# Five full-array pairs, joint normalization of two heads, bf16 beta1, alpha2 folded into the first weights, and a new order table, in a block-sparse attention and MLP kernel

## The chip, the cores and the metric

The kernel runs on one core of a Trainium2 chip. The metric is the device time of one execution in microseconds (us). The engines are TensorE (PE; PEld is its weight load), VectorE (DVE), ScalarE (ACT), GpSimd (POOL) and SyncE (SP). Before the change three runs gave 309.32, 309.18 and 308.26 us.

## What is computed

Block-sparse attention (4 batches, 8 heads, 768 tokens, head size 64, blocks of 32 tokens) is followed by a residual MLP that mixes first tokens and then channels:

```python
scores = scale * np.matmul(q, k.transpose(0, 1, 3, 2))
mask = np.abs(blk_i - blk_j) <= window      # window = 1
mask = mask | (blk_i == 0) | (blk_j == 0) | (blk_i == n_blocks - 1) | (blk_j == n_blocks - 1)
# and three sampled key blocks for each query block
scores = np.where(mask, scores, -1000000000.0)
attn = softmax(scores);  x = attn @ v        # x: [4, 768, 512], the heads side by side
a1 = alpha1 * x + beta1
u = x + lam * np.einsum('ts,bsd->btd', w_tok, a1)
a2 = alpha2 * u + beta2
out = u + lam * (np.maximum(a2 @ w_ch1, 0.0) @ w_ch2)   # w_ch1: 512 x 2048, w_ch2: 2048 x 512
```

## The kernel before, in words

**Work units.** The 32 heads form 16 pairs, four to a batch. Scores are computed transposed (keys on the partitions, queries along the free axis), in 9 units for each pair, so there are 144 units. A unit is 1024 columns in two PSUM banks. Unit n belongs to pair n // 9.

**The order table.** The whole program is the string `ORDER`. Each word is one step: letters for the kind, a number for the instance, and after a colon a PSUM bank (for `q`, a pair of banks) or an engine (`a` ScalarE, `d` VectorE). The loop at the end issues the words one after the other, `pin_order` keeps that order on every engine, and `bank_order` adds the waits between engines that reuse of a PSUM bank needs. So an engine never passes a step of its own that still waits. DMA steps stand in the queue of the engine that issues them: loads on POOL, transposes, mask and output on SP.

**Attention words.** `lq lk lv` load q, k, v of a pair with a cast to 16 bits (POOL, L402); six buffers rotate, and loads of pairs from `HELD` on wait for a flag that `F` sets on VectorE (L400). `cq ck cv` cast or regroup them (L517, L532). `q` makes the scores of a unit. For the first `NPE` = 6 pairs ("full array", L585) one head at a time is contracted over 88 rows: 64 of the head and 24 that carry the block mask, so the mask costs nothing later. Those q and k are transposed by TensorE (`H`, L335) and copied out of PSUM (`hq hk`). For the later pairs ("row-tiled", L595) the two heads of the pair run at the same time in the two halves of the array, 64 rows each. There q and k are transposed by DMA on SP's queue (`tq tk`, L554) and the mask is put on after the exp by a minimum with `maskT` on VectorE (`m`, L612). `M N O` make that mask: `N` writes it to DRAM, `O` reads it back, both on SP. `e` is the exp on ScalarE (L605), unit 0 in two halves. `p` and `r` multiply with the values of the first and the second head of the pair (L619); `n` divides by the row sums (a reciprocal, L650, and a multiplication, L653) and writes x into `x_sb`.

**Token mixing.** `lt W w` load and transpose w_tok. `a` and `b` (or by halves `ah`, `bh`) make lam * (alpha1 * x + beta1) (L674, L680). `k` is the matmul (18 of 128x128, L704), `x` adds it to x (L713).

**Channel MLP.** `u` makes alpha2 * u in bf16 (L720). `U` transposes it: by TensorE for batch 0 (L740, with `v` as the copy out of PSUM), by DMA on SP's queue after that (L734). `lw` loads w_ch1 (`w1b`), `lx` and `S` load w_ch2 and scale it by lam. `f` is one block of 128 hidden units for half a batch (four matmuls, L758); f0 to f31 belong to batch 0, whose first 16 carry beta2 along as a further column, copied into `b1t`. `g` is the relu with that bias, on ScalarE (L772) or VectorE (L774). `h` is a quarter of an output block (four matmuls, L792), `o` adds u (L802), `s` stores it (L811).

**Filling.** `z` words are matmuls with zeros into a bank that nobody reads (L298). There are 18 in the table, 7,498 columns in all, all of them ahead of f0. Seven of 512 columns and some small ones stand ahead of the table.

**The start.** Ahead of the table the first pair's q and k are cast, transposed by TensorE into banks 0 and 1, and copied out in halves by VectorE and ScalarE (the last is L359); the mask rows are made beside it.

Of the kernel before, what the change touches and what calls it, by code (L numbers as in the profile page):

```python
# [21 lines left out]
D = 64  # L22
# [3 lines left out]
DM = 512  # L26
# [11 lines left out]
NPE = 6  # L38
# [8 lines left out]
lv0 lq1 lk1 cq0 q0:1 lv1 q1:2 hm0 e0 H1:0 lq2 hq1:d e1 lk2 z512:6 z512:6 q2:1 hk1:d lt0 e2 z512:6  # L47
z512:6 q3:2 cv0 lt1 p0:7 p1 e3 q4:1 lt2 cq1 p2 e4 lv2 z393:6 q5:2 p3 lc0 e5 ck1 z422:6 q6:1 H2:0 lc1
p4 e6 q7:2 hq2:d lc2 n0 e7 z512:6 z498:6 q8:1 lq3 hk2:d r4:7 r5 lv3 e8 r6 cq2 q9:2 cv1 lk3 H3:0 ck2
e9 r7 hq3:d q10:1 lc3 r8 hk3:d e10 lc4 q11:2 n1 H4:0 lq4 W0:1 e11 hq4:d q12:1 lk4 p9:7 hk4:d p10 e12  # L50
q13:2 w0:d H5:0 e13 p11 hq5:d q14:1 p12 hk5:d e14 W1:1 q15:2 w1:d p13 W2:0 e15 n2 q16:1 W3:1 cv2 e16
r13:7 q17:2 w2:d lv4 r14 r15 w3:d e17 W4:0 lw0 L0 q18:1 lw1 r16 w4:a L1 q19:2 lw2 r17 e18 a0 W5:0
lw3 e19 n3 z512:6 z246:6 q20:1 b0 p18:7 e20 z374:6 q21:2 p19 a1 e21 z422:6 q22:1 p20 cq3 e22 z422:6
q23:2 b1 lq5 p21 e23 z422:6 q24:1 ck3 p22 cq4 lk5 H6:1 e24 n4 q25:2 lv5 hq6:d z470:6 r22:7 e25 r23
q26:1 hk6:d r24 w5:a ck4 H7:1 cv3 q27:2 lq6 hq7:d e26 r25 k0:0 lk6 hk7:d e27 cv4 q28:1 L2 lv6 H8:1
x0 e28 q29:2 lx0 hq8:d r26 k1:0 hk8:d e29 lx1 n5 q30:1 q31:2 x1 e30 H9:1 u0 p27:7 p28 hq9:d hk9:a
p29 lx2 q32:1 u1 p30 e31 k2:0 a2 e32 q33:2 M0 x2 U0:1 N0 e33 p31 q34:1 b2 k3:0 v0:a n6 q35:2 e34 x3
r31:7 r32 r33 ah6 O0 k4:0 e35 u2 bh6 q36:1 q37:2 x4 e36 r34 u3 r35 k5:0 e37 n7 q38:1 u4 q39:2 x5 e38
U1:1 ah7 p36:7 p37 v1:a u5 q40:1 p38 bh7 e39 U2:0 cq5 k6:1 v2:d lq7 e40 ck5 k7:0 B0 lk7 x6 cv5 q41:1
u6 lv7 q42:2 e41 x7 H10:1 lx3 p39 cq6 p40 hq10:a u7 z184:6 q43:1 n8 U3:0 hk10:a v3:d z189:6 r40:7  # L60
e42 r41 z384:6 H11:1 ck6 f0:0 cv6 hq11:a hk11:d q44:2 g0:d r42 e43 f1:1 S0 f2:0 e44 g1:d q45:1 g2:a
r43 q46:2 S1 tq6 tk6 r44 e45 f3:0 S2 f4:1 n9 e46 q47:1 g3:d p45:7 g4:a q48:2 a4 p46 e47 f5:0 cq7
f6:1 e48 g5:d q49:1 p47 g6:d e49 q50:2 p48 b4 f7:0 e50 q51:1 ck7 p49 g7:d k8:1 e51 n10 q52:2 tq7 tk7
q53:1 x8 e52 r49:7 r50 cv7 r51 u8 h0:6 e53 S3 q54:0 q55:2 S4 e54 r52 r53 S5 h1 e55 n11 q56:0 q57:1
e56 F24 m54 k9:4 lq8 m55 e57 p54:7 f8:5 x9 p55 m56 q58:0 q59:1 g8:a f9:4 m57 e58 p56 F25 f10:5 u9
lk8 g9:a a5 U4 p57 f11:0 g10:a f12:1 m58 g11:a f13:4 b5 p58 g12:a f14:5 g13:d h2 e59 g14:d k10:4 m59
q60:0 q61:1 cq8 x10 e60 p59 k11:5 ck8 u10 tq8 tk8 e61 f15:4 m60 x11 q62:0 q63:1 g15:a m61 p60 f16:5
e62 F26 u11 lv8 p61 f17:4 g16:a S6 e63 f18:5 g17:d m62 f19:4 g18:a m63 q64:0 q65:1 g19:a p62 S7 U5
f20:5 e64 n12 f21:4 g20:a h3 F27 m64 lq9 g21:a cv8 r54:7 r55 r56 o0 e65 r57 r58 r59 r60 r61 r62
q66:0 q67:2 s0 n13 e66 f22:2 m65 p63:7 p64 e67 f23:3 g22:d p65 h4:6 m66 g23:a m67 q68:0 q69:1 q70:2  # L70
a6 e68 p66 p67 h5 F28 e69 b6 lk9 h6 e70 m68 h7 m69 q71:0 q72:1 q73:2 m70 e71 p68 o1 p69 p70 e72 F29
h8:6 cq9 s1 lv9 m71 e73 k12:0 m72 ck9 p71 k13:1 m73 tq9 tk9 n14 f24:2 x12 r63:7 r64 g24:a r65 r66
x13 r67 r68 r69 r70 r71 ah14 f25:0 n15 h9 g25:a bh14 p72:7 q74:0 q75:1 q76:2 ah15 e74 F30 bh15 p73
lq10 h10 u12 e75 k14:0 m74 e76 u13 k15:1 x14 U6 m75 p74 f26:0 u14 p75 f27:2 g26:a x15 h11 m76 g27:a
u15 q77:0 q78:2 o2 e77 U7 p76 f28:2 F31 cv9 lk10 f29:3 e78 cq10 s2 g28:d f30:0 g29:a m77 f31:1 g30:a
m78 p77 h16:6 g31:a q79:0 q80:1 q81:2 e79 F32 p78 lv10 h17 e80 m79 f32:0 ck10 e81 p79 f33:1 m80 tq10
tk10 f34:2 g32:d g33:a p80 m81 h18 g34:a n16 q82:0 q83:1 q84:2 e82 F33 r72:7 lq11 r73 cv10 r74 r75
r76 r77 e83 r78 m82 r79 r80 f35:0 n17 e84 f36:1 g35:d p81:7 p82 g36:a f37:2 m83 f38:0 g37:a m84 p83
h19 g38:a a8 q85:0 q86:1 q87:2 o4 e85 p84 F34 h20:6 b8 s4 lk11 e86 f39:0 m85 e87 k16:1 m86 g39:a
cq11 p85 p86 m87 k17:2 x16 p87 f40:0 u16 f41:1 x17 g40:a ck11 h21 g41:a u17 tq11 tk11 h22 q88:0  # L80
q89:1 q90:2 e88 F35 h23 lv11 U8 e89 m88 f42:0 o5 f43:1 e90 p88 g42:d s5 h24:6 g43:a m89 h25 m90
q91:0 q92:1 q93:2 e91 F36 p89 lq12 h26 cv11 n18 h27 m91 r81:7 r82 o6 r83 e92 r84 r85 r86 r87 r88 r89
s6 h32:6 e93 n19 h33 m92 m93 q94:0 q95:1 q96:2 e94 a9 p90:7 p91 p92 p93 h34 e95 F37 m94 lk12 f44:0
b9 e96 p94 f45:1 g44:d q97:1 q98:2 g45:a m95 k18:0 e97 F38 m96 lv12 p95 k19:1 cq12 e98 x18 m97 p96
f46:0 x19 p97 f47:2 g46:a m98 f48:1 g47:a u18 p98 f49:0 ck12 g48:a n20 tq12 tk12 h35 g49:a u19 r90:7
r91 r92 o8 r93 r94 r95 r96 r97 cv12 r98 q99:0 q100:1 q101:2 n21 U9 e99 h36:6 F39 a10 lq13 e100 f50:0
s8 m99 h37 e101 g50:d p99:7 m100 h38 m101 q102:0 q103:1 q104:2 b10 e102 p100 p101 h39 F40 e103 lk13
m102 k20:0 o9 e104 p102 m103 k21:1 s9 x20 p103 f51:2 m104 h40:6 x21 g51:a u20 p104 q105:0 q106:1
q107:2 cq13 e105 u21 h41 F41 ck13 U10 lv13 e106 m105 f52:0 f53:1 e107 tq13 tk13 g52:d p105 f54:2
m106 g53:a h42 m107 g54:a p106 q108:0 q109:1 q110:2 e108 p107 h43 F42 lq14 n22 e109 f55:0 m108 r99:7  # L90
r100 o10 g55:a r101 r102 r103 r104 r105 r106 e110 ah22 s10 r107 f56:0 n23 h48:6 g56:a bh22 p108:7
q111:0 q112:1 q113:2 ah23 e111 m109 h49 F43 bh23 lk14 e112 p109 f57:0 m110 e113 k22:1 m111 g57:d
k23:2 x22 m112 p110 p111 f58:3 u22 p112 f59:0 g58:a x23 f60:1 m113 g59:a q114:1 q115:2 u23 g60:a
p113 cv13 f61:0 U11 e114 cq14 f62:1 ck14 g61:a m114 f63:2 tq14 tk14 g62:a h50 g63:d e115 p114 h51
# [97 lines left out]
def kernel(  # L192
# [664 lines left out]
```

## Time and profile before

| | |
|---|---|
| median of 3 runs (lowest, highest) | 309.18 us (308.26, 309.32) |
| the profiled execution | 307.76 us, its span 306.0 us |
| ScalarE: exp, 145 instructions | 139.0 us busy |
| TensorE: first layer, 512 matmuls; second layer, 371 recorded | 93.1 us; 86.7 us busy |
| VectorE: masks, 90 instructions | 60.4 us busy |
| ScalarE: relus, 104; VectorE: relus, 24 | 60.4 us; 14.8 us busy |
| loads on POOL's queue | 15.47 MB, 32.9% of the DMA engines' span |
| transposes, mask and stores on SP's queue | 14.97 MB, 23.8% |

A profile is one execution on the chip. The span runs from the first instruction to the last. "Busy" is the time in which an engine had an instruction at work; matmuls overlap, and their ends are modelled. The chain of waits starts at the last instruction and goes back, at each step to what released it. A group of instructions gives line, engine, operation, output and inputs, shape and count, then busy time and mean duration, then idle time ahead of it and who ended most of that. A table of stages gives, for each stretch of the span, the busy time of every engine (and instructions), the granted clock of TensorE as a share of full speed, the share of time that the 16 DMA engines were busy, and GB/s.

### The profile page before, as it was taken

To read this page: it belongs to the slowest core of one execution; us is meant where nothing else is said; L and a number is where in the kernel's file an instruction comes from. 1 tells how busy PE (TensorE), PEld (TensorE's weight loads), DVE (VectorE), ACT (ScalarE), POOL (GpSimd) and SP (SyncE) were. 2 spreads that over 40 slices of the span, in tenths; PEclk is the share of its full clock that TensorE was granted. 3 is DMA by queue.
4 is the path that set the end of the run, shared out by engine and by line. 5 is a ranking of instruction groups with operands and counts; after the bars stand their busy time and mean duration, and the time that the engine had idled before them with its cause. 6 is when DMAs were issued, how large, how long until landed. Compare 5 with 4: busy or idle time off the path is not lost.

```text
span 306.0 us, 7521 instructions
## 1 busy us (share of the span) xinstructions
PE 299.4 (98%) x3161; PEld 188.1 (61%) x3192; DVE 207.7 (68%) x436; ACT 205.7 (67%) x270; POOL 52.3 (17%) x91
## 2 busy tenths in 40 slices
PE   8999999999999999999999999999999999999995
PEld 3676788675654764665656664565756665555444
DVE  4689998988889986857988696889768730010112
ACT  5999987989797577855665858766758727428000
POOL 5647422102032212211222111120000000000000
PEclk9999999999999999999999999999999999999999
DMA  6999999993554677395375925475020110010021
GB/s 147 190 235 221 214 206 245 241 151 46 83 79 78 118 86 133 61 115 110 39 132 86 136 56 112 87 86 79 3 62 35 28 28 34 34 71 0 37 102 69
DMA packets 46766, 31.16 MB, mean 102 GB/s; under 512 B 27388, under 2 KB 42124, under 8 KB 46732
## 3 DMA queue, kind: packets, MB, share of 16 engines
q0 software_dynamic: 15984, 15.47, 32.9%
q1 hardware_dynamic: 30532, 14.97, 23.8%
q8 instruction: 25, 0.41, 0.5%
q10 hardware_dynamic: 216, 0.24, 0.2%
q14 instruction: 9, 0.07, 0.1%
HBM read 31.64 MB, written 7.08 MB: 127 GB/s over the span
## 4 chain that ended last, share of the span: by engine, by line
PE 92%; DMA 4%; POOL 2%; issue 1%; ACT 1%; DVE 0%
PE psum L758 27%; PE psum L792 27%; PE psum L619 12%; PE psum L704 11%; PE psum L595 7%; PE psum L585 6%; DMA wtk<-in_moe_w_tok_dram 3%; DMA q2f<-in_q_dram 1%; PE psum L335 1%; PE psum L460 1%; POOL v L402 0%; PE psum L298 0%; POOL q L402 0%; POOL k L402 0%; PE psum L740 0%
## 5 line engine op out<-in xcount | busy, mean ns | idle before, releaser
L605 ACT ACTIVATE eT<-psum 128x1024 f16<-128x1024 f32 (+1 forms) x145 | 139.0, 1021 | 36.5 <-PE psum L595 27.6
L758 PE MATMUL psum<-uT,w1b 128*128 128x384 bf16 (+1 forms) x512 | 93.1, 326 | 0.1
L792 PE MATMUL psum<-w2b,hts 128*128 128x512 bf16 (+1 forms) x371 | 86.7, 370 | 1.6 <-issue 0.2
L772 ACT ACTIVATE hts<-psum,b1t 128x384 bf16<-128x384 f32 x104 | 60.4, 583 | 37.4 <-PE psum L758 33.4
L612 DVE TENSOR_TENSOR eT<-eT,maskT 128x1024 f16<-128x1024 f16 x90 | 60.4, 687 | 17.7 <-ACT eT L605 17.2
L758 PEld LDWEIGHTS <-w1b 128*128 128x128 bf16 x512 | 46.4, 98 | 28.8 <-ACT eT L605 0.8
L619 PEld LDWEIGHTS <-eT 128*128 128x128 f16 x1152 | 49.0, 97 | 20.2 <-issue 4.0
L792 PEld LDWEIGHTS <-hts 128*128 128x128 bf16 x400 | 36.6, 98 | 36.2 <-issue 1.8
L619 PE MATMUL psum<-vext,eT 128*128 128x65 f16 x1152 | 56.2, 193 | 0.0
L802 DVE TENSOR_TENSOR ot<-x_sb,psum 128x512 f32<-128x512 f32 (+1 forms) x25 | 16.6, 664 | 50.9 <-PE psum L792 50.9
L704 PE MATMUL psum<-a1p,wtokT 128*128 128x128 bf16 x576 | 36.6, 219 | 0.0
L704 PEld LDWEIGHTS <-wtokT 128*128 128x128 bf16 x576 | 33.3, 98 | 2.9 <-ACT eT L605 0.4
L585 PE MATMUL psum<-qx,kx 88*128 88x512 bf16 (+1 forms) x144 | 31.4, 326 | 0.1
L400 POOL COPY held<-flag 1x1 bf16<-1x1 bf16 x24 | 9.4, 391 | 121.3 <-DVE flag L419 121.3
L595 PE MATMUL psum<-qx,kx 64*128 64x512 bf16 (+1 forms) x240 | 25.6, 326 | 0.0
L713 DVE TENSOR_TENSOR x_sb<-x_sb,psum 128x384 f32<-128x384 f32 x32 | 17.5, 551 | 4.0 <-PE psum L704 3.4
L653 DVE TENSOR_TENSOR x_sb<-psum,rcp 128x384 f32<-128x384 f32 x32 | 17.8, 558 | 1.1
L720 DVE TENSOR_TENSOR ub<-x_sb,a_bc 128x384 bf16<-128x384 f32 x32 | 17.7, 552 | 0.1
L595 PEld LDWEIGHTS <-kx 64*128 64x128 bf16 x240 | 8.9, 94 | 13.4 <-issue 4.5
L774 DVE TENSOR_SCALAR hts<-psum,b1t 128x384 bf16<-128x384 f32 x24 | 14.8, 616 | 2.2 <-PE psum L758 1.2
L680 DVE TENSOR_TENSOR a1p<-a1p,b_bc 128x768 bf16<-128x768 bf16 (+1 forms) x20 | 15.8, 792 | 0.1
L674 DVE TENSOR_TENSOR a1p<-x_sb,a_bc 128x768 bf16<-128x768 f32 (+1 forms) x20 | 15.8, 792 | 0.1
(62 smaller groups left out, 149.2 us busy)
## 6 DMA issues: line engine op xcount, KB each, us to landing
out_dram<-ot SPq DMA_DIRECT2D x23, 256.0 KB, 2.0
v<-in_v_dram POOLq DMA_DIRECT2D x16, 192.0 KB, 5.4
q<-in_q_dram POOLq DMA_DIRECT2D x15, 192.0 KB, 4.9
k<-in_k_dram POOLq DMA_DIRECT2D x15, 192.0 KB, 4.7
w1b<-in_moe_w_ch_dram POOLq DMA_DIRECT2D x4, 512.0 KB, 10.0
w2b<-in_moe_w_ch_dram POOLq DMA_DIRECT2D x4, 512.0 KB, 13.9
wtk<-in_moe_w_tok_dram POOLq DMA_DIRECT2D x3, 384.0 KB, 9.9
mask_rows<-maskT SPq DMA_DIRECT2D x1, 768.0 KB
```

The lines of the kernel that those rows point to most:

```text
L585: nc.tensor.matmul(t[:, f : f + w], kx[h][0:KC, ts(jt, P)], qx[h][0:KC, c : c + w], start=True, stop=True,)
L595: nc.tensor.matmul(t[:, a * 512 + f : a * 512 + f + w], kx[h][r, ts(jt, P)], qx[h][r, c : c + w], start=True, stop=True,)
L605: nc.scalar.activation(eTs[n][:, c], t[:, c], AF.Exp, bias=EXPB, scale=SCALE)
L612: nc.vector.tensor_tensor(out=e, in0=e, in1=mask, op=ALU.min)
L619: nc.tensor.matmul(ops[p, a][:, t * VW : t * VW + D + 1], eTs[n][:, c : c + P], vext[p % NV][:, a, jt, 0 : D + 1], start=(jt == t == 0), s ...
L653: nc.vector.tensor_tensor(out=x_sb[:, s0 : s0 + NT, h * D : (h + 1) * D], in0=t[:, :, 0:D], in1=rcp[:].unsqueeze(2).broadcast_to([P, NT, D ...
L704: nc.tensor.matmul(t[:, j, :], wtokT[:, s, ts(3 * g + j, P)], a1p[p][:, s, :], start=(s == 0), stop=(s == NT - 1),)
L713: nc.vector.tensor_tensor(out=sl, in0=sl, in1=tps.pop(i), op=ALU.add)
L720: nc.vector.tensor_tensor(out=ub[p][:, 3 * g : 3 * g + 3, :], in0=x_of(p, 3 * g, 3, 0, P), in1=per_col(a2_bc, p, 3, 0, P), op=ALU.mult,)
L758: nc.tensor.matmul(hps[i][:, 0:w], w1b[:, dk, ts(f, P)], uT[b][:, dk, hf * HS : hf * HS + w], start=(dk == 0), stop=(dk == 3),)
L772: nc.scalar.activation(hts[kk][:, f, :], t[:, 0:HS], AF.Relu, bias=b1t[:, f : f + 1], scale=1.0)
L792: nc.tensor.matmul(cps[i][:, 0:w], hts[kk][:, nk, ts(m, P)], w2s[0][:, nk, lo : lo + w], start=(nk == 0), stop=(nk == 15),)
```

## The change

- **NPE from 6 to 5.** Pair 5 goes from the full array to the row-tiled form: H10, H11 and their copies go; tq5, tk5 and the masks m45 to m53 come. `HELD` follows, from 8 to 7.
- **Two heads normalized together.** For row-tiled pairs the values of both heads stand in two neighbouring banks, and one `n` does both heads: a reciprocal of 12 columns and a multiplication of 768.
- **beta1 in bf16.** lam * beta1 is written to a bf16 tile, so that `b` reads 16-bit inputs only.
- **alpha2 in the first weights.** `P0` to `P7` multiply eighths of `w1b` by alpha2 (one scalar for each partition), in place, on ScalarE or VectorE, after batch 0 has used them. From batch 1 on `u` is then a plain copy to bf16, on either engine.
- **Casts on either engine.** `cq ck cv` take an engine: 15 of them go to ScalarE.
- **A new table.** It has no `z` words. Of the relus 72 are on ScalarE and 56 on VectorE (104 and 24 before). The first score units come in the order 1, 0, 3, 2; scores use all four pairs of banks; the loads are in another order.

Code edits:

```diff
-NPE = 6
+NPE = 5
...
-            nc.vector.tensor_mul(out=t[:], in0=t[:], in1=lam_bc[:])
+            t, to = ((a1_bc, a1_bc), (b1_bc, b1_bcb))[i]
+            nc.vector.tensor_mul(out=to[:], in0=t[:], in1=lam_bc[:])
...
-        nc.vector.tensor_copy(out=dst, in_=by_head(ld.pop((p, i))[:]))
+        copy(eng, dst, by_head(ld.pop((p, i))[:]))
...
-                ops[p, a] = bank(bank_, [P, 512])
+                ops[p, a] = bank(2 * bank_ + a if p >= NPE else bank_, [P, 512])
...
+        if p >= NPE:
+            del ops[p, 0], ops[p, 1]
+            t = psum[:, ts(ov[p], UN)].rearrange("p (a c) -> p a c", a=2)[:, :, 0 : NT * VW]
+            t = t.rearrange("p a (t w) -> p a t w", t=NT)
+            rcp = wk.tile([P, 2, NT], FP, name="rcp", tag="rcp", bufs=2)
+            nc.vector.reciprocal(out=rcp[:], in_=t[:, :, :, D])
+            nc.vector.tensor_tensor(
+                out=x_of(p, 0, NT, 0, P).rearrange("p t (a d) -> p a t d", a=2),
+                in0=t[:, :, :, 0:D],
+                in1=rcp[:].unsqueeze(3).broadcast_to([P, 2, NT, D]),
+                op=ALU.mult,
+            )
+            return
...
-        nc.vector.tensor_tensor(out=t, in0=t, in1=per_col(b1_bc, p, NT, c, w), op=ALU.add)
+        nc.vector.tensor_tensor(out=t, in0=t, in1=per_col(b1_bcb, p, NT, c, w), op=ALU.add)
...
+        dst, src = ub[p][:, 3 * g : 3 * g + 3, :], x_of(p, 3 * g, 3, 0, P)
+        if p >= NPAIR:
+            copy(eng, dst, src)
+        else:
+            nc.vector.tensor_tensor(out=dst, in0=src, in1=per_col(a2_bc, p, 3, 0, P), op=ALU.mult)
...
+    @on("P")
+    def _(i, eng):
+        g, dk = divmod(i, 4)
+        w = w1b[:, dk, ts(g, FF // 2)]
+        if eng == "a":
+            nc.scalar.mul(w, w, a2T[:, dk : dk + 1])
+        else:
+            nc.vector.tensor_scalar(out=w, in0=w, scalar1=a2T[:, dk : dk + 1], scalar2=None, op0=ALU.mult)
```

Stretches of the new table that the prediction speaks of: the start; around q29; from k7 to q48; P6 and f47; the end of pair 15; the last transpose; the end.

```
lv0 lk1 lq1 q1:0 cq0 hm0 F21 q0:2 q3:1 lq2 e1 lk2 H1:6 e0 e3 lt1 q2:0 hk1:d hq1:d F22 lt0 q4:2 q5:3
...
p18:7 hq7:d x0 q30:0 r24 lk6 lk4 lw1 lw2 a1 u0 L2 b1 M0 F23 u1 ck4:d q27:2 cq4:d e30 lq7 q28:1
r25 q29:0 p19 e28 p20 e29 lc4 p21 r26 q31:1 p22 lc5 n5 n4 e27 e31 lq6 cv3:d lx1 lx2 k3:0 cv4:d x3
...
p29 r32 p30 v0:a lv7 k2:3 hq8:d b2 hk8:a e35 lk5 x2 p31 e34 n6 q36:3 k5:0 cq7:a e36 B0 q39:1 lv5 lx0
...
k6:3 u4 e38 e41 x6 e42 k7:2 u6 x7 q40:0 p36:4 U2:3 p37 e40 u7 v2:d S3 S2 ck5:d p38 U3:5 q43:0 q44:3
p39 v3:a r40:5 e43 e44 f0:3 f7:2 f4:1 f2:0 f5:6 g0:a g7:a tk5 f6:7 g2:a g5:a g6:a p40 ck7:d tq5 n8
f9:3 f12:6 f18:7 N0 f16:4 g9:d g4:a g12:a g18:d S5 S4 f10:1 f14:0 f15:3 g10:a g14:a g16:d r41 g15:d
r42 q48:3 q52:0 F25 f8:2 r43 r44 lk8 e48 lx3 F26 e52 f11:3 n9 g8:a q47:0 q53:3 g11:d cq8:d q51:2
f20:2 e51 O0 a4 f23:3 e53 e47 g23:d f3:4 g3:d lv8 cq6:d F27 f13:5 tq7 f1:3 f21:1 f22:0 b4 f19:4 S7
...
P4:d h16:2 m72 m76 m80 cq14:d h17 h18 cv10:a U7 q74:0 q91:3 q73:2 P6:d m79 F45 lv14 h19 f52:3 s6 e74
lq15 m77 f47:0 f42:1 m74 e91 e73 g47:a f44:6 p72:2 m73 f34:7 f45:0 o4 g44:d m75 g42:d ck14:d F46
...
s14 r128 r129 p131 r130 p132 p133 r131 p134 r132 r133 r134 h89 n28 h90 a14 h91 q140:3
q138:1 q137:0 b14 o22 e138 k29:4 e140 k28:5 x29 m136 e137 x28 m138 m140 h80:7 q141:1 q142:2 u28:d
e141 q143:0 h81 q139:1 h84:6 m135 u29:d u24:d e142 U12 U14 s22 m141 m137 e139 m139 m142 p135:2 s17
e143 m143 h85 p136 r135 p137 r136 p138 r137 p139 p140 r138 p141 r139 r140 p142 r141 p143 r142 r143
h82 n30 h86 a15 h72:2 b15 h87 k31:3 k30:0 x31 u31:d x30 u30:d U15 o21 h83 h73 h74 h75 o18 s21 f104:0
...
h125 s24 o28 h121 h122 h126 h123 h127 s28 o30 o31 s30 s31
```

## The prediction

> **What bounds the kernel now.** I read the page first: busy shares, slices, chain.
>
> ```profile
> span 306.0 us, 7521 instructions
> ...
> PE 299.4 (98%) x3161; PEld 188.1 (61%) x3192; DVE 207.7 (68%) x436; ACT 205.7 (67%) x270; POOL 52.3 (17%) x91
> ...
> PEclk9999999999999999999999999999999999999999
> ...
> PE 92%; DMA 4%; POOL 2%; issue 1%; ACT 1%; DVE 0%
> ```
>
> TensorE is the chain: 92%, at full clock. Since the ends of matmuls are modelled, 98% busy may hide waits, so I took the pieces of the chain, whose lengths are those of a gap-free stream (start, length, what; two stretches):
>
> ```profile
> 37.30 0.87 PE psum L585 x5
> 38.16 0.34 PE psum L335 x6
> 38.50 0.73 PE psum L619 x24
> ...
> 115.89 0.86 PE psum L792 x4
> 116.75 0.76 PE psum L595 x8
> ```
>
> Two full-array score units cost 0.87, six transposes 0.34, 24 value matmuls 0.73, four second-layer matmuls 0.86, a run of three row-tiled units 0.76 (a run of two: 0.54). The same chain has 0.65 for four first-layer and 1.00 for 18 token-mixing matmuls; the start times add 0.10 ahead of each row-tiled run. So a row-tiled unit is 0.22 and a run costs 0.20 beside its units. Counted over the table: first layer 128 x 0.65 = 83.2; second layer 82.6; mixing 32.0; values 1152 x 1.09/36 = 34.9; 21 groups of six transposes 7.1; 54 full units 23.5; 35 row-tiled runs (20 of three, 15 of two) 15.2 + 8.1 + 3.5 = 26.8; zero matmuls 7,498 columns at 0.43 ns = 3.2. Sum **293.3 us**. The first score matmul starts at 6.49 and the last second-layer matmul ends at 303.0, so TensorE waited only 303.0 - 6.5 - 293.3 = **3.2 us** in all that time: 0.5 on the token weights at 17.1, most of the rest before 30. Only less work on TensorE can shorten this kernel, as long as nobody else falls behind.
>
> Who could? The busy times by stage (PE, PEld, DVE, ACT, POOL, clock, DMA share, GB/s):
>
> ```profile
> 10.00:15.00 5.00, 4.94 (x72) 3.32 (x69) 2.96 (x8) 5.00 (x6) 2.66 (x5) 1.00 1.23 205
> 20.00:25.00 5.00, 5.00 (x85) 4.08 (x82) 4.59 (x10) 4.99 (x6) 3.04 (x5) 1.00 1.16 257
> 25.00:30.00 5.00, 4.91 (x65) 3.19 (x65) 4.97 (x10) 5.00 (x7) 3.77 (x7) 1.00 1.25 217
> 40.00:45.00 5.00, 5.00 (x88) 4.45 (x86) 4.65 (x11) 5.00 (x6) 1.48 (x2) 1.00 1.30 200
> ```
>
> Until the first layer starts (55.97 in the timeline) ScalarE, VectorE and the DMA engines are full too. After 120 VectorE is at 60 to 90%, and from 250 on nearly idle.
>
> **The change, part by part.** *Order table and pair 5.* On TensorE the zero matmuls go (-3.2); pair 5 leaves 9 full units (-3.9) and two transpose groups (-0.7) and adds 9 row-tiled ones: 37 runs (26 of three, 10 of two, 1 of one) are 19.8 + 5.4 + 0.3 + 3.7 = 29.2, +2.4. Together **-5.3**, to 288.0. Around it: four PSUM copies go (three on ScalarE, 0.8 each), 9 masks come (9 x 0.687 on VectorE), and two DMA transposes on SP's queue, ahead of the mask's write and read. POOL gets three more flag copies (0.39 each) and the load of a2T (0.84 as be2T), where its queue has idle time: nothing.
>
> *Other VectorE and ScalarE work*, from these groups (busy us, mean ns):
>
> ```profile
> L612 DVE TENSOR_TENSOR eT<-eT,maskT 128x1024 f16<-128x1024 f16 x90 | 60.4, 687 | 17.7 <-ACT eT L605 17.2
> L653 DVE TENSOR_TENSOR x_sb<-psum,rcp 128x384 f32<-128x384 f32 x32 | 17.8, 558 | 1.1
> L720 DVE TENSOR_TENSOR ub<-x_sb,a_bc 128x384 bf16<-128x384 f32 x32 | 17.7, 552 | 0.1
> L680 DVE TENSOR_TENSOR a1p<-a1p,b_bc 128x768 bf16<-128x768 bf16 x12 | 11.4, 952 | 0.0
> L517 DVE COPY rel<-q 128x768 bf16<-128x768 bf16 x15 | 5.3, 356 | 0.6 <-DMA q<-in_q_dram 0.6
> L330 DVE CAST rel<-q2f 128x384 bf16<-128x384 f32 x2 | 0.7, 361 | 2.7 <-DMA q2f<-in_q_dram 2.6
> ```
>
> Adding beta1 with only 16-bit inputs lies between 0.95 (L680) and 768/1024 of L612, 0.52; it has L612's form, and I take 0.55. Normalizing two heads at once lies between one 768-element pass (0.95, L674) and two of L653 (1.12), with one or two reciprocals of 0.19; I take 0.95 + 0.20, against 1.50. The plain u copy lies between L330 (0.36) and L720 (0.55); I take 0.45. Scaling the first weights on VectorE lies between a copy (0.356 x 1024/768 = 0.47) and L612 (0.69), I take 0.47; on ScalarE 1.03 as the exp of this size. VectorE's sum: masks +6.2, 32 relus moved to it at 0.616 +19.7, 15 casts moved away -5.3, beta1 -6.7, normalizing -3.8, u -4.6, five weight scalings +2.4, the rest nothing: +8, to 216 (70%). ScalarE: relus -18.7, casts +12.4, u +2.6, three scalings +3.1, PSUM copies -4.1: -5, to 201. None of this sets the end by itself; TensorE's 288 covers it, and where the cover is thin it is priced below.
>
> [...] L330 ran fast with 384 in and 64x6 out. [...]
>
> *The wait on the scaled weights.* Batch 1's first-layer matmuls (f52, then f47) wait for the scalings, and each scaling for batch 0's last use of its block, some 35 us of TensorE work earlier. The last one, P6, stands in VectorE's queue 1.5 of TensorE's work (h19, f52) ahead of f47, behind masks and with m79 and m77 behind it; the values of pair 8 wait for those. TensorE's work hides it: nothing, unless VectorE is over 1.0 late there; then f47 waits for the rest, and f44, f34 with it.
>
> *The start.* Units 1 and 0 change places, and unit 1 writes banks 0 and 1, which ScalarE reads until 6.93 (L359): first score at 6.95, not 6.49 (**+0.46**). The first exp is now a whole unit, at 7.6, not 6.95. Exps follow each other 0.92 apart. Unit q29 takes the banks that e30 frees, the 28th exp in the table, with one cast (0.7) ahead of it: 7.6 + 28 x 0.92 + 0.7 + 0.1 = 34.2. TensorE's words before q29 (30 units, 7 transpose groups, 25 value steps, 6 weight groups, 2 mixings) end at 6.95 + 24.9 = 31.8. So TensorE waits for ScalarE, where the zero matmuls stood: **2.3**; 1.9 at the shortest spacing seen (0.904), 3.3 if ScalarE idles 0.5 in two stages, as in 15 to 20 (4.52 busy). The same sum for the table of before gives a lag of 0.3.
>
> *Later covers.* The u transposes of pairs 11 and 15 have four second-layer steps behind them, 4 x 0.86 = 3.4. In the trace of before the last such chain runs from k's end at 246.43 (x, u, DMA 2.7) to about 250.4, 4.0: **+0.5 each**. Pair 15's last masks: from x28 to m143 VectorE has eight masks at 0.60 start to start, one x at 0.47 and three u at 0.36, 6.4, with latencies 6.7; TensorE's work there is 6.7: 0 to 0.6, taken as **+0.2**. The last stores stand closer: SP issues of 0.3 to 0.5, **+0.4**. Of before's own waits the 0.5 on the token weights goes (their DMA is issued earlier), the others before 30 fall together with ScalarE's, **1.3** stay. Waits: 2.3 + 1.0 + 0.2 + 0.4 + 1.3 = **5.2**. Bounds: 1.9 (ScalarE's lag alone) and 8.9 (3.3, 1.4 with slow u copies, 0.6, 0.4, and all 3.2 of before).
>
> **Sum.** 6.95 + 288.0 + 5.2 + 3.0 (last output and store, as before) = **303.2 us** of span against 306.0, -2.8. The profiled execution took 307.76, the median of the runs 309.18. The profiled one is 1.4 under the median; I set the difference against the median: **306.4 us**.
>
> **Rivals.** *Pair 5's transposes come late (slower).* The table loads pair 5's k as the 35th load; with it 9,092 KB of loads have to pass.
>
> ```profile
> q0 software_dynamic: 5695, 6.30, 75.7%
> ...
> qx<-rel SPq DMA_TRANSPOSE x2, 11.4
> kx<-rel SPq DMA_TRANSPOSE x2, 11.8
> ```
>
> That is the stretch 30 to 80: under the load queue's traffic a transpose landed after 11 to 12 us; the whole run's k median is 2.9. At the 200 to 260 GB/s of the stages pair 5's k lands near 52. TensorE gets to q48 at 6.95 + 51.3 + 2.8 = 61. Transposes issued at 52.3 and 55.4 land at 55 to 58 if free, at 64 to 67 if slow as before. For: nothing can pass q48 on TensorE. Against: in before the 768 KB mask read was issued 1.2 us ahead of them on the same queue; here it comes after. The price is 6; it decides once the second lands after 61: 306.4 + 6 = **312.4**. [...]
>
> *All is given back (no change).* Between k1 and the first f the table asks 23.0 us of VectorE per 23.1 of TensorE; before, 25.7 per 27.3, or 94%, went without a gap. At 94% the 23.0 need 24.5, +1.4; the stage of pair 7 (11.4 per 10.0) loses another 1.3 likewise: 306.4 + 2.7 = **309.1**. For: VectorE's 4.97 of 5 above. Against: VectorE may work ahead there.
>
> *All is kept:* no waits beyond before's 3.2 less the 0.5: 6.95 + 288.0 + 2.7 + 3.0 = 300.7, -5.3: **303.9**. Against: ScalarE's lag above.
>
> That the clock drops without the zero matmuls I price at nothing: it was 1.00 in every stage, and the longest wait I expect is 2.3, in parts.
>
> **Chances.** Forecast 0.55 (its own range 304.5 to 308), no change 0.24, slower 0.13, all kept 0.08. A half per cent, 1.5 us, is what a measurement tells from no change. Faster: 0.45 of the forecast, all kept 0.08, 0.05 of no change = 0.58; the same: 0.10 + 0.17 = 0.27; slower 0.13 + 0.02 = 0.15. Range 302.5 (just under 303.0, the sum with waits of 1.9) to 311.5 (most of the late transposes).
>
> **What would show it.** First layer's start near 53.5 to 54.5 (55.97 before); q48 with no wait on a DMA; row-tiled runs of 0.76; L680's successor near 0.55; f104 waiting about 0.5 on the last uT. Wrong if TensorE waits over 8 us in all, or if ScalarE has idle time before 30.

## The result, and the profile after

The changed kernel took **312.88 us** (four runs, 312.11 to 315.75), the kernel before 308.93 in the runs beside it: a ratio of 1.015, interval [1.012, 1.019]. It is slower by 1.5%; 306.4 had been forecast, inside a range that ended at 311.5. Six more runs later gave 313.05, ratio 1.016 [1.013, 1.019]. The profiled execution was the longest of the first four: 315.75, span 314.0.

First its page: span, busy time by engine, granted clock in 40 slices, chain of waits.

```profile
span 314.0 us, 7397 instructions
...
PE 298.1 (95%) x3138; PEld 186.4 (59%) x3162; DVE 216.9 (69%) x434; ACT 198.7 (63%) x260; POOL 51.9 (17%) x95
...
PEclk9999999999879999999999999999999999999998
...
PE 62%; DMA 21%; DVE 10%; ACT 4%; issue 2%; SPq 0%; POOL 0%; DVEq 0%
```

TensorE had 92% of the chain before; now it has 62%, and DMA went from 4% to 21%. VectorE (216.9) and ScalarE (198.7) are where they were forecast (216, 201). The clock line has an 8 and a 7 in slices 11 and 12 that were not there before (the last 8 stands behind the last matmul). So more of the time went to waits on transfers, and these two slices are the place to look. The stages there (PE, PEld, DVE, ACT, POOL, clock, DMA share, GB/s):

```profile
75.00:80.00 5.00, 3.71 (x33) 1.88 (x33) 4.92 (x11) 3.82 (x7) 0.02 (x1) 1.00 1.34 103
80.00:85.00 5.00, 2.21 (x20) 0.96 (x17) 3.54 (x8) 2.04 (x3) 3.93 (x7) 0.84 1.31 179
85.00:90.00 5.00, 4.78 (x59) 3.49 (x58) 2.37 (x7) 1.94 (x2) 1.07 (x3) 0.50 1.17 140
```

TensorE was idle for 4.1 us of the first ten, and then had half its clock (0.50 from 85 to 90). TensorE's waits from 50 to 130 (who waited for whom, us, times, longest):

```profile
PE psum L598 <- DMA qx<-rel: 2.8, 1, 2.8
PE psum L722 <- DVE flag L421: 1.4, 1, 1.4
PE psum L822 <- DVE w2b L480: 0.7, 1, 0.7
PE psum L822 <- DVE hts L804: 0.6, 1, 0.6
PE psum L788 <- DMA w1b<-in_moe_w_ch_dram: 0.5, 1, 0.5
```

L598 is the first row-tiled unit of pair 6 (q56) and waits for its transposed q; L822 is the second layer's first step (h0) and waits for w2b's scaling and, behind it on VectorE, a relu; L788 is f0; L722 is k14, the mixing of pair 7, at 122. Now the queues, from the timelines of POOL, VectorE and SP (start, length, instruction; in brackets the idle time ahead of it and its releaser):

```profile
30.74 0.72 POOL L404 DMA_DIRECT2D k<-in_k_dram  x1 [5.23 <-DVE vext L388]
31.45 1.10 POOL L446 DMA_DIRECT2D w1b<-in_moe_w_ch_dram  x2
...
64.31 0.18 POOL L402 COPY held<-flag 1x1 bf16<-1x1 bf16 x1 [14.72 <-DVE flag L421]
64.79 0.72 POOL L404 DMA_DIRECT2D k<-in_k_dram  x1 [0.30 <-issue]
65.50 0.76 POOL L452 DMA_DIRECT2D w2b<-in_moe_w_ch_dram  x1
```
```profile
73.39 1.90 DVE L480 TENSOR_TENSOR w2b<-w2b,lam_bcb 128x1024 bf16<-128x1024 bf16 x3 [2.69 <-DMA w2b<-in_moe_w_ch_dram]
75.20 1.14 DVE L804 TENSOR_SCALAR hts<-psum,b1t 128x384 bf16<-128x384 f32 x2
76.25 0.68 DVE L480 TENSOR_TENSOR w2b<-w2b,lam_bcb 128x1024 bf16<-128x1024 bf16 x1
```
```profile
60.28 0.84 SPq L502 DMA_DIRECT2D mask_rows<-maskT  x1
67.92 0.36 SPq L509 DMA_DIRECT2D maskT<-mask_rows  x1
68.46 1.38 SPq L557 DMA_TRANSPOSE qx<-rel  x1
69.89 8.96 SPq L557 DMA_TRANSPOSE kx<-rel  x2
```

The same three in the kernel before, the first of the w1b loads, the last quarter of w2b and the mask's write:

```profile
25.84 0.58 POOL L443 DMA_DIRECT2D w1b<-in_moe_w_ch_dram  x1
53.56 0.77 POOL L449 DMA_DIRECT2D w2b<-in_moe_w_ch_dram  x1
40.97 0.82 SPq L499 DMA_DIRECT2D mask_rows<-maskT  x1
```

POOL stands still twice: 5.2 us for a tile buffer (the first-layer weights w1b stand behind that load) and 14.7 us for a flag, with the last quarter of w2b (`lx3`) behind it. `lx3` was issued at 53.56 in the kernel before, at 65.50 here; the w1b loads at 25.84 to 28.4 before, at 31.45 to 40.8 here; the mask's write at 40.97 before, at 60.28 here. VectorE waits 2.7 us for `lx3`, with relus behind it. On SP two transposes take 8.96 us to issue, from 69.89 on, while the mask is read (issued at 67.92, landed 10.1 us later). The share of time in which the DMA engines are busy is 0.20 from 70 to 75 in the kernel before and 0.42 to 0.70 from there to 95; here it stays between 1.1 and 1.4 from 70 to 95.

Where the lateness arises is seen best as a running sum: the start of each TensorE step, less the start it would have in a gap-free stream by the prediction's prices, from the first score on. (The first profile lacks 24 matmuls, so the first column is from the second profile of the changed kernel, span 311.8; the other columns are kernels of the next section.)

| lateness (us) at | changed | e19 | e10 | e9 | e17 |
|---|---|---|---|---|---|
| first layer, f0 | 4.6 | 3.3 | 5.4 | 4.5 | 3.6 |
| second layer, h0 | 5.3 | 7.9 | 7.0 | 4.5 | 3.6 |
| pair 6, q56 | 8.4 | 10.3 | 6.9 | 5.4 | 3.7 |
| values of pair 5, p45 | 9.8 | 10.4 | 7.0 | 5.6 | 3.8 |
| mixing of pair 7, k14 | 11.3 | 11.3 | 8.8 | 7.3 | 4.1 |
| last step | 13.2 | 13.2 | 10.6 | 9.2 | 6.0 |

Each column adds up to its span: for the changed kernel 6.6 + 287.9 of work + 13.2 + 4.1 from the last matmul to the end = 311.8.

### The profile page after: what moved, and what is told of

The parts are those of the page before. It is cut to its first block, busy times and chain, and to the rows that moved or that the text cites. A ratio compares the mean times of both kernels' runs of the same rounds, so it can differ in the third digit from the quotient of the medians.

```text
span 314.0 us, 7397 instructions
## 1 busy us (share of the span) xinstructions
PE 298.1 (95%) x3138; PEld 186.4 (59%) x3162; DVE 216.9 (69%) x434; ACT 198.7 (63%) x260; POOL 51.9 (17%) x95
## 4 chain that ended last, share of the span: by engine, by line
PE 62%; DMA 21%; DVE 10%; ACT 4%; issue 2%; SPq 0%; POOL 0%; DVEq 0%
PE psum L788 22%; PE psum L822 19%; PE psum L622 8%; PE psum L598 6%; PE psum L722 5%; DMA w1b<-in_moe_w_ch_dram 4%; DMA maskT<-mask_rows 3%; DVE eT L615 3%; ACT eT L608 3%; DMA mask_rows<-maskT 2%; DMA q<-in_q_dram 2%; DMA kx<-rel 2%; DMA uT<-ub 2%; DMA qx<-rel 2%; DMA k<-in_k_dram 2%
## 5 line engine op out<-in xcount | busy, mean ns | idle before, releaser
L608 ACT ACTIVATE eT<-psum 128x1024 f16<-128x1024 f32 x145 | 138.5, 1021 | 47.3 <-PE psum L598 42.3
L822 PE MATMUL psum<-w2b,hts 128*128 128x512 bf16 (+1 forms) x376 | 86.9, 372 | 3.1 <-issue 1.0
L788 PE MATMUL psum<-uT,w1b 128*128 128x384 bf16 (+1 forms) x512 | 89.1, 326 | 0.7 <-DMA w1b<-in_moe_w_ch_dram 0.5
L788 PEld LDWEIGHTS <-w1b 128*128 128x128 bf16 x512 | 48.3, 98 | 35.1 <-issue 1.9
L802 ACT ACTIVATE hts<-psum,b1t 128x384 bf16<-128x384 f32 x72 | 40.2, 583 | 40.5 <-PE psum L788 39.2
L822 PEld LDWEIGHTS <-hts 128*128 128x128 bf16 x400 | 36.6, 98 | 41.3 <-issue 5.9
L804 DVE TENSOR_SCALAR hts<-psum,b1t 128x384 bf16<-128x384 f32 x56 | 33.7, 615 | 24.8 <-PE psum L788 23.9
L622 PEld LDWEIGHTS <-eT 128*128 128x128 f16 x1152 | 43.6, 99 | 10.5 <-DVE eT L615 1.6
L622 PE MATMUL psum<-vext,eT 128*128 128x65 f16 x1152 | 46.9, 195 | 0.5 <-issue 0.2
L722 PE MATMUL psum<-a1p,wtokT 128*128 128x128 bf16 x576 | 36.0, 219 | 1.7 <-DVE flag L421 1.4
L722 PEld LDWEIGHTS <-wtokT 128*128 128x128 bf16 x576 | 33.2, 98 | 6.1 <-issue 3.1
L598 PE MATMUL psum<-qx,kx 64*128 64x256 bf16 (+1 forms) x264 | 28.7, 332 | 2.8 <-DMA qx<-rel 2.8
L588 PE MATMUL psum<-qx,kx 88*128 88x512 bf16 (+1 forms) x120 | 25.1, 326 | 1.1 <-DVE flag L421 0.4
L598 PEld LDWEIGHTS <-kx 64*128 64x128 bf16 x264 | 10.4, 95 | 17.8 <-issue 6.7
L404 POOL DMA_DIRECT2D v<-in_v_dram x16 | 11.6, 724 | 13.4 <-ACT rel L386 6.2
L588 PEld LDWEIGHTS <-kx 88*128 88x128 bf16 x120 | 9.7, 97 | 6.6 <-ACT eT L608 1.8
L404 POOL DMA_DIRECT2D q<-in_q_dram x15 | 10.7, 713 | 10.5 <-DVE flag L421 5.3
```

The source lines that it names most:

```text
L404: nc.gpsimd.dma_start(t[:], pair_ap(src, *batch(p)))
L588: nc.tensor.matmul(t[:, f : f + w], kx[h][0:KC, ts(jt, P)], qx[h][0:KC, c : c + w], start=True, stop=True,)
L598: nc.tensor.matmul(t[:, a * 512 + f : a * 512 + f + w], kx[h][r, ts(jt, P)], qx[h][r, c : c + w], start=True, stop=True,)
L608: nc.scalar.activation(eTs[n][:, c], t[:, c], AF.Exp, bias=EXPB, scale=SCALE)
L622: nc.tensor.matmul(ops[p, a][:, t * VW : t * VW + D + 1], eTs[n][:, c : c + P], vext[p % NV][:, a, jt, 0 : D + 1], start=(jt == t == 0), s ...
L722: nc.tensor.matmul(t[:, j, :], wtokT[:, s, ts(3 * g + j, P)], a1p[p][:, s, :], start=(s == 0), stop=(s == NT - 1),)
```

## Experiments

**What the removed zeros were worth** (e3). The kernel before, all `z` words out of its table.

> The kernel before, its order table without the zero matmuls (7,498 columns, 3.2 us of TensorE), and nothing else. Theory 'they stood in waits': before 45 ScalarE's exps set the pace, TensorE then waits where the zeros stood, and the time stays within 0.7 of 308.9. Rival 'they cost their length': 305.7, 3.2 less. Rival 'they kept the clock': without them the granted clock falls below 0.97 in some stage before 50 and the time is over 310.

308.38 (ratio 1.000 [0.997, 1.002]), clock 1.00 in every stage looked at (5 to 150). They stood in waits. TensorE's longest waits of the first 60 us that came with it:

```profile
PE psum L584 <- ACT eT L604: 1.4, 4, 0.5
...
PE psum L618 <- DVE x_sb L652: 0.7, 1, 0.7
```

So of the 5.3 us of TensorE work that the change removes, 3.2 were never on the path by themselves; the forecast had charged 2.3 of them back as ScalarE's lag.

**First theory: the mask on SP's queue** (e1), with the end (e2) and the clock (e4) beside it.

```diff
e1: - ... f18:7 N0 f16:4 ... e51 O0 a4 ...     + ... b1 M0 N0 O0 F23 ...
e2: - ots[i] = wk.tile([P, DM], FP, name="ot", tag="ot", bufs=2)
    + ots[i] = wk.tile([P, w], FP, name="ot", tag="ot" if w == DM else "oth", bufs=2)
e4: - ... q56:1 ...     + ... (14 times z512:2) q56:1 ...
```

> The mask's write and read (N0, O0) move in the order table from the 60s of the trace to right behind the row of mask bits (M0); nothing else changes. Theory 'mask on SP's queue': in the changed kernel the write is issued at 60.28 and the read at 67.92, the transposes of pairs 7 and 6 stand behind them on SP's queue, and TensorE waits 7.3 us between 75 and 90 for what they make late. Then the wait of 3.0 at 81.2 goes, the granted clock is at least 0.97 in every 5 us stage, and the time falls from 312.9 by 4 to 7, to 306 to 309. Rival 'load traffic': the stage is slow because 11.4 MB have to pass between 30 and 95, wherever the mask stands; then the waits between 75 and 90 stay within 2 us of what they were and the time is 311 to 313.

317.24, 4 us slower still: both theories missed. The wait on pair 6's transposes did go, but w1b landed at 59.3:

```profile
PE psum L788 <- DMA w1b<-in_moe_w_ch_dram: 5.2, 1, 5.2
PE psum L822 <- DVE hts L804: 1.2, 1, 1.2
```

The mask's 1.5 MB came at the cost of the weights. The mask was only one of several transfers in a stretch that was too full.

> The two half-width output tiles of the last row blocks (o30, o31) get two buffers of their own, so that they no longer wait for the stores of o24 and o28. Theory 'output buffers': in the changed kernel 7.0 us pass from the end of the last matmul (307.05) to the end of the span, 3.05 in the kernel before; here o28, o30 and o31 run back to back, the 7.0 becomes about 4.6, and the time falls by 2.4, to about 310.5. Rival 'SP's queue': the stores' own issues set the end; then it falls by less than 0.7.

312.75 (310.1 to 314.6): no gain that can be told from the scatter. The expectation also had its number wrong: 307.05 was the end of an earlier step, the last matmul of that profile ended at 309.66. So 4.3 us, not 7.0, lie behind it, against 3.05 before; 3.4 to 3.5 were left with the separate buffers (e2, e9, e17).

> The changed kernel with 14 zero matmuls of 512 columns (3.0 us) put into the wait at 81.2 (ahead of q56, into the banks that q56 overwrites), so that TensorE works there although the transpose is as late as before. Theory 'the wait lowers the clock': the granted clock was 0.50 from about 83.7 to 90.1 in the profiled execution; with the wait filled it stays at 1.00 there, TensorE's stretch after it runs at full rate, and the time falls by 1.5 to 3, to 310 to 311.4. Rival 'the clock falls by itself, from load or heat': it is 0.50 there still and the time stays at 312 to 313.5.

Where the wait was filled, the clock stayed up:

```profile
80.00:85.00 5.00, 4.93 (x43) 2.48 (x43) 5.00 (x12) 3.87 (x5) 2.09 (x4) 1.00 1.44 117
85.00:90.00 5.00, 5.00 (x54) 2.59 (x53) 2.21 (x6) 2.36 (x3) 1.85 (x4) 1.00 1.26 213
```

But the times came in two groups, 310.0 and 310.9 against 314.5 and 314.7, median 312.67. In the profiled one (314.65) the full clock came only at 17.4 us; ahead of 6 in the other profiles until then. So the median doesn't show the 1.5 to 3 us that were expected; the stages do show 1.00 from 80 to 90, where the changed kernel had 0.84 and 0.50. The late first clock is taken up under "the start" below.

**Second theory: the order of the loads** (e5; with the early mask e6; with everything e8).

```diff
- ... lk6 lk4 lw1 lw2 ... lq7 ... lq6 ... lk7 lw3 lw0 ... lx0 lq8 ... lk8 e48 lx3 ...
+ ... lk6 lw1 lw2 lk4 lw3 ... lq7 ... lq6 lw0 ... lk7 ... lx0 lx3 lq8 ... lk8 e48 ...
```

> Only the order of POOL's load queue is changed: the first-layer weights' loads lw1 and lw2 stand ahead of lk4 (whose tile buffer is freed late: POOL idles from 25.5 to 30.7 in the changed kernel), lw3 behind lk4, lw0 behind lq6, and the last quarter of the second-layer weights (lx3) behind lx0, ahead of the flag that held it until 65.5. Theory 'load order': the weights stand behind loads that wait for buffers; then POOL's gap at 25 to 31 goes, the first layer starts without a wait on w1b (0.7 before), the second layer's waits on w2b's scaling near 75 (1.6) go, and the transposes of pairs 5 to 7 come some us earlier, so that the wait of 3.0 at 81 shrinks: 309 to 311. Rival 'bandwidth': the DMA engines have no room, the order only moves the waits from one tile to another, and the time stays at 312 to 313.5.

**308.94** over ten runs, 4 us less, ratio to the kernel before 1.004 [1.000, 1.007]. No wait of over 0.5 is left between 50 and 110. One has come, 2.4 us near 38, on pair 4's k, which now stands behind the weights.

> The load order of the run before this one, and the mask's write and read early, as in e1_mask_early. There the early mask took away the wait on pair 6's transposes, but w1b landed 4.8 us later (59.3) and the first layer waited 5.4. Theory 'load order': with w1b ahead there is room for both, no TensorE wait of over 1 us is left between 50 and 100, and the time is 306.5 to 309. Rival 'bandwidth': the mask's 1.5 MB come at the cost of another load, and the time is 311 or more.

313.41: the rival. Pair 5's q came late this time (q48), the place of the prediction's slow rival:

```profile
PE psum L598 <- DMA qx<-rel: 3.2, 1, 3.2
```

> Everything together: load order, early mask, buffers of their own for the last two outputs, the six zero matmuls of the start. By the theories the parts add: the 4.3 us of waits between 75 and 84 in the changed kernel, 0.7 at the first layer, 2.4 at the end, and no lowered clock: 312.9 less 7 to 9, 304 to 306, under the kernel before. Rival: the waits move to the next late tile and it is 307 or more.

311.65, the same wait at q48 (2.7 in its profile). Of the two places tried for the mask, the late one of the change is the better.

**Which load** (e10: `lx3` alone; e19: w1b alone; e16: the changed kernel again).

> The changed kernel with one load moved: the last quarter of the second-layer weights (lx3) ahead of the flag that held it. Tells which of the moved loads of e5_loads counted. If it was this one: the waits at 75 (1.6) go and the time falls by 1.5 or more, to 311.4 or less. If it was the first-layer weights: the first layer still waits 0.7, pair 6's transpose still 2 to 3, and the time stays within 1 of 312.9.

> The changed kernel with only the first-layer weights' loads moved (lw1 behind lk6; lw2, lw3 behind lk4; lw0 behind lq6); lx3 stays behind its flag. If the moved loads add up: e10_lx3_only gave 3.2, both together 4.1, so this gives about 1: 311.5 to 312.5, no wait at 54, and those at 75 to 84 as in the changed kernel. Rival 'either one makes the room': it gives 2.5 or more by itself, 310.5 or less.

> The changed kernel itself, unchanged, for its scatter. By the theories its spread has two parts: the first full clock (late in one execution of five to ten) and the lowered clock after the wait at 81; median 312 to 313.5, lowest 310.5, highest 316.

313.05 for e16, 309.83 for e10, 314.10 for e19. `lx3` alone is worth 3.2 us. The weights of the first layer alone gain nothing (1.0 slower, which their scatter of 312.7 to 317.0 does not set apart): f0 comes in time, TensorE reaches the second layer earlier, and there `lx3` is as late as ever. VectorE's wait for it, with e10's issue on POOL below:

```profile
76.10 1.90 DVE L480 TENSOR_TENSOR w2b<-w2b,lam_bcb 128x1024 bf16<-128x1024 bf16 x3 [6.61 <-DMA w2b<-in_moe_w_ch_dram]
```
```profile
50.02 0.74 POOL L452 DMA_DIRECT2D w2b<-in_moe_w_ch_dram  x1 [1.74 <-DMA w2b<-in_moe_w_ch_dram]
```

In e10 the last quarter is issued at 50.0 instead of 65.5, VectorE has no wait for it, SP's two transposes take 5.5 instead of 8.6 to 9.0 us, and pair 6 no longer waits. It isn't free: in e10's profile f0 waits 1.9 us for w1b (0.5 and 0.7 in the changed kernel), and q48 waits 1.5 for pair 5's q, so the 3.2 is what is left of a larger gain. In e19 TensorE waits 4.5 at h0, and the mean clock of that execution is 0.989 (1.000 in e10's). e19's expectation failed, sum and rival: the moved loads don't add up, since a gain ahead of the late load is lost at it.

**Putting it together** (e9; e13 and e17 with more zeros at the start).

```diff
e9:  + as e5, but  lk6 lw1 lk4 lw2 lw3 ;  cv2:d ahead of a0 ;  h122 h123 h126 h127 ;  tile "oth" as in e2
e13: + as e9, zero(P, 6) 8 and 16 times around the first transposes (2 and 7 before)
e17: + as e9, 5 and 14 times;  ck13:d behind b7
```

> e5_loads, whose only wait of over 0.8 us was 2.4 at 37.8 (the load of pair 4's k, now behind 1 MB of first-layer weights, landed at 37.96), with one 512 KB load less ahead of it (lw2 behind lk4), pair 4's buffer freed earlier (cv2 ahead of a0 on VectorE), and the end of e2_end (own buffers for the last two outputs; h123 ahead of h126). Theory 'load order and end': the wait at 38 falls below 1, the end from 4.0 to about 3.5 us behind the last matmul; 308.9 less 1.5 to 3: 306 to 307.4, under the kernel before. Rival: another load comes late in place of pair 4's k, and it stays at 308 or more.

**307.24**, 0.997 [0.994, 1.000] of the kernel before: as expected.

> e9_best with more zero matmuls ahead of the first score: 8 in place of 2 before the transposes, 16 in place of 7 behind them (15 x 128 columns). In two of ten profiles the clock was granted in full only at 13.8 and 17.4; ahead of 5.9 the others. Theory 'idle time between 4.3 and 6.7 makes some executions miss the full clock at the start': then no execution is over 1.5 us above the fastest, where e9_best has one or more of six 3 to 5 us above. Rival: late executions are as frequent in both. The median may be up to 0.3 higher for the six matmuls ahead of the transposes.

307.14 (306.09 to 308.31), where e9 spread from 306.3 to 310.2. One of twelve lies 2.2 above the fastest, the others within 1.5, so nearly as the theory had it; the test is weak, since e9 had only two of twelve more than 2.2 above its fastest.

> e9_best with 5 in place of 2 zero matmuls ahead of the first transposes and 14 in place of 7 behind them (e13_warm, trimmed), and with the cast of pair 13's k (ck13) behind a7 and b7 on VectorE's queue: in e13_warm VectorE waited until 114.2 for that load (issued at 110.0) with a7 and b7, which the mixing of pair 7 needs at 116, queued behind. Theory 'VectorE's order': TensorE's wait at 116 (0.6 to 1.5) goes, and the time is 305.5 to 306.8. Rival 'late load': pair 13's k is then late for something else and it stays at 307 or more.

**306.39** (305.55 to 307.35), **0.995 [0.993, 0.997]** of the kernel before: faster than that one and than the changed one. The wait at k14 is gone, as 'VectorE's order' had it. Its page:

```profile
span 304.3 us, 7439 instructions
...
PE 297.7 (98%) x3172; PEld 185.5 (61%) x3172; DVE 216.7 (71%) x434; ACT 198.3 (65%) x260; POOL 52.2 (17%) x95
...
PEclk9999999999999999999999999999999999999999
...
PE 85%; DVE 9%; ACT 2%; DMA 2%; issue 1%
```

**The parts priced at nothing** (e12, e14, e15: e9 with parts undone).

```diff
e14: - in1=per_col(b1_bcb, ...)   + in1=per_col(b1_bc, ...)     (beta1 and its product with lam in fp32)
e15: - if p >= NPAIR: copy(eng, dst, src)     + tensor_tensor(out=dst, in0=src, in1=per_col(a2_bc, ...))
     - the eight P words
e12: both
```

> e9_best with two parts of the change undone: beta1 in fp32 (its 15 pair-wide adds 0.95 instead of 0.55 us), and alpha2 multiplied into u for all batches on VectorE (24 plain copies become products of 0.55, the 8 scalings of the first weights go). By the prediction VectorE's and ScalarE's sums are off the path that sets the end: within 0.7 of e9_best, at most 1 more at the last transposes. Rival 'VectorE's cover is thin': 12 us more on VectorE delay masks and mixing, 1.5 us or more.

> e9_best with beta1 kept in fp32, alpha2 as changed. Undoing both parts cost 3.6 us. Theory 'VectorE's time ahead of the mixing': the adds (b words) stand directly ahead of the token mixing (k words) on VectorE's queue, which TensorE waited for in e9_best (1.45 at 116.9) and longer in e12_undo_small (2.0); then this undoing alone costs 1.5 us or more, 308.7 to 310.5. Rival 'alpha2': below 0.7, at most 308.

> e9_best with alpha2 multiplied into u for all batches on VectorE and the 8 scalings of the first weights left out; beta1 in bf16 as changed. [...] Theory 'beta1': within 0.7 of e9_best, 306.5 to 308. Rival 'alpha2': 1.5 or more above it.

310.82 for both, 310.17 for beta1 alone, 307.82 for alpha2 alone, against 307.24. The bf16 beta1 is worth **2.9 us** in this table, alpha2 in the weights nothing that can be told (intervals to before: [0.997, 1.001] and [0.994, 1.000]). In e14 TensorE waits 2.2 us at k14, against 1.3 in e9, and the rest comes in small waits ahead of other mixings.

**The start** (e7: zeros where TensorE waits; e18: the start's zeros on half the rows).

```diff
e7:  + z512:7 z512:7 q4:2 ... z512:3 z256:3 q8:0 ... z512:4 z512:4 p4
e18: - warm[:, 0:P], warm[:, 0:w]     + warm[0:D, 0:P], warm[0:D, 0:w]     (in zero, on e9)
```

> The changed kernel with six zero matmuls (2,816 columns, 1.2 us) put back where TensorE waits between 8.8 and 14.1, in banks that are free there. Theory 'late full clock': in the profiled execution of e4_fill the clock was granted in full only from 17.4 on, in the others from 4 to 6 on, and that execution took 4 us more than the fastest one of the same kernel; the zeros of the kernel before kept TensorE busy there. Then the full clock comes by 6 in the profile, and the times lie within 1.5 us of each other, at 310 to 312. Rival 'scatter of another kind': the times still spread over 3 us or more and the median is 312 to 313.5.

311.73, spread from 310.6 to 317.1, full clock at 13.8 in the profile (eight score matmuls from 6.81 on took 2.77 us, five from 11.72 on 1.91): the theory that idle time there is to blame fell.

> e9_best with its zero matmuls ahead of the first score (7 x 512, 9 x 128 columns) on 64 rows of the array in place of 128; they last as long. [...]

310.15, all ten between 309.8 and 311.4: 2.9 over e9. TensorE's timeline of e18, then the same two rows of e9:

```profile
1.19 3.38 PE L300 MATMUL psum<-warm 64*128 64x512 bf16 x9 [1.19 <-DVE warm L297]
...
7.23 2.74 PE L588 MATMUL psum<-qx,kx 88*128 88x512 bf16 x8
```
```profile
1.19 3.27 PE L300 MATMUL psum<-warm 128*128 128x512 bf16 x9 [1.19 <-DVE warm L297]
...
6.57 1.59 PE L588 MATMUL psum<-qx,kx 88*128 88x512 bf16 x8 [0.31 <-DVE qx L357]
```

The zeros take as long in both, and the same first eight score matmuls 2.74 us in the one and 1.59 in the other. The two kernels differ in the rows of the zeros alone, so here the 2.9 us come with the rows, and not with the time that the zeros keep TensorE busy.

## Why the prediction was wrong, step by step

- **The bound and TensorE's work: right.** The price list gives 287.9 for the changed table (288.0 forecast), and with the waits it adds up to the span.
- **Prices of single operations: right, one at its bad end.** From the groups of the changed kernel:

```profile
L698 DVE TENSOR_TENSOR a1p<-a1p,b_bcb 128x768 bf16<-128x768 bf16 x15 | 8.3, 555 | 0.3
L659 DVE TENSOR_TENSOR x_sb<-psum,rcp 128x768 f32<-128x768 f32 x11 | 10.5, 957 | 0.4
L753 DVE TENSOR_SCALAR w1b<-w1b,a2T 128x1024 bf16<-128x1024 bf16 x5 | 2.4, 479 | 0.0
L388 DVE CAST ub<-x_sb 128x384 bf16<-128x384 f32 x19 | 10.2, 548 | 0.1
```

  0.555 (0.55 forecast), 0.957 (0.95), 0.479 (0.47); the u copy (128x3 in, one run of 384 out) 0.548 where 0.45 was taken: as long as the product before (0.552, L720), while L330 with 384 in and 64x6 out took 0.361. The 1.4 with slow u copies in the prediction's bounds puts 0.2 more on each of two transposes; no run shows that term by itself. What the runs showed is copies of 0.548, and 1.9 of lateness from k14 to the last step, where 1.2 had been set.
- **The start: right in size.** First score at 6.6 to 6.7 (6.95). Up to 38 TensorE waited 3.6, where 2.3 for ScalarE and 1.3 kept from before had been set. The cause fits too: in the second profile ScalarE works from 7.5 to 36.9 with 0.4 us of idle time, and q29 starts at 35.0 (34.2).
- **The step that failed: the loads of the new order.** The prediction costed POOL's side as "three more flag copies ... and the load of a2T ..., where its queue has idle time: nothing", and of the loads after the start it followed pair 5's k alone. The table moves `lx3` from 53.6 to 65.5, w1b by 5 to 12 us, and the mask by 19 us. In the second profile of the changed kernel this cost 0.9 at f0, 1.5 at h0 and the step behind it, 2.4 at q56 and 1.3 of lowered clock, 6.1 in all (lateness 3.7 ahead of f0, 9.8 at p45). Moving the loads back took 4.1 (e5), and `lx3` alone 3.2 (e10). Of the 8.6 us by which that profile's span (311.8) exceeds the 303.2 of the sum, the rest is mainly 1.5 from p45 to k14 (VectorE stands 0.6 for the load of pair 13's k ahead of k14's input; in e17, with that cast behind b7, the 1.5 is 0.3), 0.7 more than set in the covers behind it, and 0.6 more at the end. TensorE waited 13.2 in all, so the prediction's own sign of being wrong, over 8 us, came true.
- **The slow rival: right mechanism, wrong place.** DMA transposes late on SP's queue were its subject, at pair 5 (q48) and for 6 us. In the changed kernel q48 waits for nothing; pair 6 waits 2.4 to 2.8, with SP's issues for it behind the mask's read. So it is chance that the rival's 312.4 lies near the measured 312.9. At q48 the wait came in e6 and e8 (3.2, 2.7), where the mask was early, and in e10 (1.5), where `lx3` was.
- **The clock, "priced at nothing": wrong.** Behind the wait at 81 it was 0.50 for 6.8 us in one profile (83.45 to 90.27) and for 3.4 in the other (0.92 and 0.74 in the stages 80 to 85 and 85 to 90): at most an estimated 2.9 and 1.7 us of TensorE's time, half of the 5.76 us that it was busy there and half of the 3.4. The waits were 2.8 and 2.4 us, where at most 2.3, in parts, had been expected, and TensorE was still busy for 2.21 and 2.59 of the 5 us from 80 to 85.
- **"None of this sets the end by itself": wrong for beta1.** Its 0.4 us per pair stand directly ahead of the mixing on VectorE's queue and are worth 2.9 (e14); right for alpha2 (e15).
- **The no-change rival**, VectorE late ahead of f0: not seen; lateness grew by 0.2 between k1 (29.7) and the last step ahead of f0.
- **The end**: 0.4 forecast, 1.0 to 1.3 measured, as the last two outputs wait for buffers.

What the forecast describes is the kernel with its loads in time: waits of 5.2 set, 6.0 in e17, which took 306.39. That it is so near to 306.4 is partly chance, since e17 also has a repaired end, more zeros at the start and two casts moved on VectorE, and since its span, 304.3, is 1.1 over the 303.2 of the sum: the difference had been set against a median 1.4 above the profiled run. Not settled: how much of the 3.2 of `lx3` comes by way of VectorE's queue, and how much by its 512 KB no longer sharing the DMA engines with the mask's read; both changed at once in e10, and so did the hold of SP's queue (5.48 us, against 8.96 and 8.56 in the changed kernel).

## What to carry to other kernels

When the order of a kernel changes, write down for every transfer, on every queue, its issue before and after, what gates it (a buffer, a flag, the issue ahead of it) and its first use; a load behind somebody else's gate is late by that gate (here POOL stood still for 14.7 us with `lx3` behind it). A transfer pulled forward in a full stretch pushed another out (e1: a wait of 5.2 us for w1b; e6: 3.2 for pair 5's q; in part e10: 1.9 and 1.5), and a gain ahead of a late load was lost at that load (e19: 314.10, against 313.05), so repair the last late one first. Matmuls with zeros that stood in waits cost nothing and brought nothing by their removal (e3: 308.38, ratio 1.000).

## Unexpected on the hardware

- **Zeros on half the rows, and a slower start.** In e18, with the zeros on 64 rows, the zeros took 3.38 us (e9: 3.27), the first eight score matmuls behind them 2.74 (1.59), and eight from 10.40 on still 2.88 (in e9 four from 8.41 on 0.88); no execution came within 2.5 us of e9's median. The full clock came late in two other profiles, at 17.4 in e4 and 13.8 in e7, without much idle time ahead of it: in e4 TensorE was busy for 2.00 of each 2 us from 4 to 18, and in e7 it had no gap from 6.81 to 13.4, mostly on 88-row scores, of which the first eight took 2.77 us. What decides when the full clock comes is not shown by these runs.
- **The half clock lasted 6.8 or 3.4 us** in mid-kernel, in the four profiles whose stages show it: 6.8 in the changed kernel's first (0.50 from 83.45 to 90.27) and in e1 (0.71 and 0.61 from 55 to 60 and 60 to 65), 3.4 in the changed kernel's second (0.92 and 0.74 from 80 to 85 and 85 to 90) and in e6 (0.94 and 0.72 from 65 to 70 and 70 to 75). A wait of nearly the same length had it behind it in one profile and not in another: 2.4 us at q56 in the second profile of the changed kernel did, 2.7 at q48 in e8, with 1.00 in every stage from 5 to 125, did not.
- **DMA transposes held SP's queue.** A pair of them (kx) took 5.17 (e5) to 8.96 us (the changed kernel's first profile) to issue beside the mask's read, and 2.61 to 2.74 in e1, e6 and e8, where the mask's read had been issued 19 to 22 us before.
